# Turnings of x spread over the second layers, mixed blocks placed behind two doubles, a range check in two steps

## The chip, the cores and the metric

The kernel runs on one core of one Trainium2 chip. The metric is the device time of one execution in microseconds. Experiments that were sent together ran on one chip, beside runs of the kernel before on that chip; there were three such calls, on three chips.

## The reference

Causal attention with a learned decay bias over 8 batches, 8 heads, 576 tokens and head width 64, whose output (4608 tokens of width 512) goes through a top-1 mixture of 8 experts, each a two-layer network of width 1024:

```python
attn = softmax(scale * q @ k.T + min(-(cum_i - cum_j), 0), causal)
x = (attn @ v), heads joined                # (8, 576, 512)
for b in range(B):
    for s in range(S):
        fresh_e = argmax(x[b, s] @ w_gate)
        e = fresh_e if s == 0 or local_gate[b, s] < 0.5 else prev_e
        p = softmax(x[b, s] @ w_gate)
        out[b, s] = p[e] * (relu(x[b, s] @ w1[e]) @ w2[e])
        prev_e = e
```

All numbers are float32.

## The kernel before

The kernel first does attention (to about 302 us), sorting tokens by expert on the way, and then the expert stage, which is all that the change touches. Tokens of one expert are fetched in units: a "double" of 256 rows, a "single" of 128, or a "mixed" unit of two halves of 64 rows with two experts. The order of units is fixed; which expert a unit has is read from tables. There are 12 doubles (two of them "early", at the start), 10 singles and 4 mixed units.

```python
ORDER = "DMDSDMSDSDMSDSDMSDSDSDSS"
...
def turn_x(i, k):                       # transpose 128 rows of x
    x = xg.pop((i, k))
    ps = ps_x.tile([P, DK, P], F32, name="xp")      # pool of ONE buffer
    for c in range(DK):
        tr(ps[:, c, :], x[:, ...], ident)
    ...
    nc.vector.tensor_copy(xT[i][:, :, k * P : k * P + P], ps)
...
def layer1(i, first, last):
    ...
                else:                                # a mixed unit: 16 matmuls for each of 8 f
                    for swap in range(2):
                        for c in range(DK):
                            for h in range(2):
                                ...
                                mm(y[d, m], lhsT=w[h ^ swap][:, c, ...], rhs=xT[i][:, c, m], ...)
                for _ in range(nbs[i]):
                    tick()                           # counts steps; fires the hooks
...
def layer2(i, k, then):
    ps = ps_y.tile([P, D], F32, name="yp")
    for c in range(FK):                              # 8 chunks
        ...mm(ps, lhsT=hT[i][:, c, ...], rhs=wn[:, c, :], ...)
        if c == FK // 2 - 1:
            then()
        tick()
    y = gp.tile([P, D], F32, name="y", bufs=3)
    nc.vector.tensor_scalar_mul(y, ps, gate[i, k])
    nc.gpsimd.indirect_dma_start(out=..., in_=y, ...)

def turn(i):
    for k in range(2):
        turn_x(i, k)

def second(i):
    for k in range(nbs[i]):
        layer2(i, k, (lambda: turn_x(i + 2, k)) if nbs[i] == 2 else (lambda: turn(i + 2)))
...
turn(0)
layer1(0, 0, 4)
turn(1)
layer1(0, 4, FK)
...
for i in range(2 if ready else 0, NU):
    load(i)
    layer1(i + 1, 0, 4)
    fetch(i + 3)
    layer1(i + 1, 4, FK)
    second(i)
```

The first layer of unit i+1 comes before the second layer of unit i, and the rows of unit i+2 are turned inside the latter. Beside this, work of other kinds hangs on counted steps ("hooks"): the tail of attention and the first part of the last sorting at step 2, later parts at steps 6 to 16, and at step 60 a check that no softmax sum was out of range (three VectorE instructions, a matmul that adds over partitions, four small instructions).

Each float32 `mm` of the layers becomes two weight loads and two matmuls on the tensor engine (PE): in the trace the four mixed first layers, 4 x 128 calls, have 1024 weight loads and 1024 matmuls. So "x8" of a layer in a view stands for four calls, and a mixed first layer of 128 calls for 512 instructions.

## Time and profile before

| | |
|---|---|
| time | 882.5 us median (878.65 to 883.48, 3 runs) |
| time, with the run beside the kernel after | 880.58 us median (877.19 to 883.48, 4 runs) |
| span of the profiled run | 885.9 us |
| PE busy | 97% of the span |
| granted clock of PE, mean | 0.992 |
| DMA queue of instructions | 57 packets, 0.93 MB |

In the views, PE is the tensor engine's matmuls, PEld its weight loads, DVE VectorE, ACT ScalarE and POOL GpSimd. "PE hp L1129 <- issue: 7.0, 4, 3.7" means that PE, before the matmuls of line 1129 that write hp, waited 7.0 us in 4 waits, the longest 3.7, for nothing that the profile shows. In the chain of waits in order of time the columns are start, length and what ran. "hp" is a first layer, "yp" a second layer, "xp" the transposes of x, "bank" small matmuls of the hooks. A "block" is 256 instructions of PE, read from the traces: 57 packets of 16 KB came for the 14,268 instructions that the trace of the kernel before has of PE and its sequencer (250 each).

### The profile page before, as it was taken

What the parts mean: (1) busy time and instruction counts of PE and PEld (TensorE: products, weight loads), DVE (VectorE), ACT (ScalarE), POOL (GpSimd) and SP (SyncE); (2) the same over time, 40 slices, a digit from 0 to 9 for tenths busy, and PEclk for the clock granted to TensorE, in tenths of its full rate; (3) what the DMA queues carried; (4) which work ended last, traced back from release to release, by engine and by line L of the source; (5) the groups of instructions that cost most, each with busy time, mean ns of one, the idle gap of its engine ahead of it and who ended that gap; (6) DMA issues with size and microseconds to landing.
All of it is one profiled execution on the core that took longest, in us unless ns stands there. A gap on an engine that the chain in (4) does not pass through costs nothing.

```text
span 885.9 us, 17609 instructions
## 1 busy us (share of the span) xinstructions
PE 855.4 (97%) x7051; PEld 595.1 (67%) x7051; DVE 313.5 (35%) x837; ACT 185.4 (21%) x493; POOL 189.8 (21%) x289
## 2 busy tenths in 40 slices
PE   9999999999999999899998999999999999999996
PEld 7777776776767775486666567666667657676763
DVE  3656775778686665201111111111111111111110
ACT  5555555555455200000000000000000000000000
POOL 4322336237254114101010100101010101111000
PEclk9999999999999999999999999999999999999999
DMA  9165046653452518996797489776987689776000
GB/s 305 38 195 157 32 162 228 239 160 125 148 169 85 198 44 293 386 408 202 234 393 261 160 307 389 258 234 212 335 315 233 225 295 377 273 242 234 30 25 27
DMA packets 61403, 191.24 MB, mean 216 GB/s; under 512 B 7965, under 2 KB 9277, under 8 KB 61312
## 3 DMA queue, kind: packets, MB, share of 16 engines
q1 hardware_dynamic: 52272, 159.27, 52.1%
q0 software_dynamic: 8896, 30.47, 9.1%
q8 instruction: 57, 0.93, 0.4%
q10 hardware_dynamic: 144, 0.29, 0.1%
q14 instruction: 34, 0.28, 0.1%
HBM read 166.76 MB, written 23.76 MB: 215 GB/s over the span
## 4 chain that ended last, share of the span: by engine, by line
PE 93%; DVE 3%; issue 2%; POOL 1%; ACT 0%; POOLq 0%; DVEq 0%
PE yp L1146 30%; PE hp L1122 26%; PE ps L305 10%; PE o L353 10%; PE b L384 4%; PE o L377 4%; PE hp L1129 4%; PE xp L1097 2%; PE idle L269 1%; DVE xT L1100 1%; DVE r_u L921 0%; POOL x_rows L986 0%; DVE r_v L922 0%; ACT sc L311 0%; PE bank L917 0%
## 5 line engine op out<-in xcount | busy, mean ns | idle before, releaser
L1146 PE MATMUL yp<-w,hT 128*128 128x512 f32 (+1 forms) x480 | 202.0, 598 | 1.4 <-issue 1.4
L311 ACT ACTIVATE sc<-ps,bias 128x320 f32<-128x320 f32 (+4 forms) x448 | 160.5, 465 | 121.2 <-issue 62.9
L1122 PE MATMUL hp<-xT,w 128*128 128x128 f32 (+1 forms) x1088 | 172.2, 318 | 0.8 <-DVE xT L1100 0.8
L1122 PEld LDWEIGHTS hp<-xT,w 128*128 128x128 f32 x1088 | 157.5, 191 | 20.1 <-issue 7.8
L1146 PEld LDWEIGHTS yp<-w,hT 128*128 128x128 f32 (+1 forms) x480 | 79.8, 181 | 90.3 <-issue 88.4
L1153 POOL DMA_INDIRECT out_dram<-y,at x38 | 38.6, 1016 | 469.4 <-DVE y L1152 461.7
L1137 ACT ACTIVATE hT<-hp 128x512 f32<-128x512 f32 x38 | 22.7, 597 | 529.1 <-PE hp L1122 465.6
L305 PE MATMUL ps<-qk 64*128 64x320 f32 (+4 forms) x896 | 110.4, 380 | 3.6 <-DVE r_v L922 3.1
L1135 DVE TENSOR_SCALAR hT<-hp 128x512 f32<-128x512 f32 x38 | 26.2, 690 | 226.0 <-PE hp L1122 189.2
L353 PE MATMUL o<-sc,va 128*64 128x320 f32 (+4 forms) x896 | 101.3, 365 | 0.0
L317 POOL TENSOR_SCALAR_AFFINE_SELECT sc<-sc 128x256 f32<-128x256 f32 (+1 forms) x96 | 60.1, 626 | 152.5 <-ACT sc L311 103.6
L305 PEld LDWEIGHTS ps<-qk 64*128 64x128 f32 x896 | 72.2, 188 | 27.0 <-issue 7.0
L1146 PE MATMUL yp<-x,hT 128*128 128x512 f32 (+1 forms) x192 | 87.1, 604 | 0.0
L353 PEld LDWEIGHTS o<-sc,va 128*64 128x64 f32 x896 | 57.1, 137 | 42.7 <-issue 18.7
L1152 DVE TENSOR_SCALAR y<-yp,gate 128x512 f32<-128x512 f32 x38 | 28.5, 750 | 121.3 <-PE yp L1146 121.3
L1122 PE MATMUL hp<-xT,x 128*128 128x256 f32 x320 | 70.1, 380 | 0.0
L1122 PEld LDWEIGHTS hp<-xT,x 128*128 128x128 f32 x320 | 60.6, 190 | 11.1 <-issue 3.1
L340 DVE TENSOR_TENSOR sum<-sum,sc 128x640 f32<-128x640 f32 (+2 forms) x96 | 61.2, 637 | 9.8 <-POOL sc L317 4.9
L1100 DVE COPY xT<-xp 128x512 f32<-128x512 f32 x38 | 26.2, 691 | 101.7 <-PE xp L1097 101.6
L1146 PEld LDWEIGHTS yp<-x,hT 128*128 128x128 f32 (+1 forms) x192 | 34.1, 184 | 37.7 <-issue 37.6
L384 PE MATMUL b<-turn,xT 128*64 128x146 f32 x566 | 51.5, 291 | 0.6 <-issue 0.6
L986 POOL DMA_INDIRECT x_rows<-x,r_slot_i x40 | 43.4, 1086 | 11.4 <-issue 8.8
(156 smaller groups left out, 568.0 us busy)
## 6 DMA issues: line engine op xcount, KB each, us to landing
w<-in_w_dram SPq DMA_DIRECT2D x184, 512.0 KB, 7.1
x<-in_w_dram SPq DMA_DIRECT2D x56, 512.0 KB, 5.5
qk<-in_q_dram SPq DMA_DIRECT2D x32, 288.0 KB, 3.8
va<-in_vm_dram SPq DMA_DIRECT2D x35, 256.0 KB, 5.0
qk<-in_k_dram SPq DMA_DIRECT2D x31, 288.0 KB, 4.9
xg<-x_rows POOLq DMA_DIRECT2D x30, 293.0 KB
x_rows<-r_empty SPq DMA_DIRECT2D x6, 293.0 KB, 4.2
xg<-x_rows SPq DMA_DIRECT2D x4, 293.0 KB, 4.9
```

What stands on the lines that cost most here:

```text
L305: mm(ps[:, h, at : at + z - a], lhsT=kb[d, hp, KEYS[c] : KEYS[c] + P], rhs=qb[d, hp, a:z], start=True, stop=True)
L311: nc.scalar.activation(sc[:, h, at : at + z - a], ps[:, h, at : at + z - a], Act.Exp, bias=bias[:, i : i + 1], scale=scale)
L317: nc.gpsimd.affine_select(out=x, in_=x, compare_op=Alu.is_ge, fill=0.0, base=0, pattern=[[0, 2], [0, len(diag)], [1, P]], channel_multipli ...
L340: add(x, x, piece(n, c, 1), op=Alu.add)
L353: mm(o[DH * h : DH * h + DH, a - q0 : z - q0], lhsT=vas[b % 2][:, c, 2 * hp + h, :], rhs=w[:, h], start=(c == 0), stop=(c == (1, NF)[g]))
L377: mm(xs["o", 1][p : p + TL, i : i + 1], lhsT=w, rhs=one, start=True, stop=True)
L384: mm(ps[p : p + TL, t * 2 * HW : (t + 1) * 2 * HW], lhsT=xs["t", g][:, a : a + TL], rhs=w, start=True, stop=True)
L986: self.s.nc.gpsimd.indirect_dma_start(out=next(self.s.views)[:, :], out_offset=bass.IndirectOffsetOnAxis(ap=self.slot[:z, m : m + 1], axis=0),
L1122: mm(y, lhsT=w[0][:, c, f : f + P], rhs=xT[i][:, c, :], start=(c == 0), stop=(c == DK - 1))
L1129: mm(y[d, m], lhsT=w[h ^ swap][:, c, f + h * HALF : f + h * HALF + HALF], rhs=xT[i][:, c, m], start=(c == 0), stop=(c == DK - 1))
L1146: mm(ps[n * m : n * m + m, :], lhsT=hT[i][:, c, a : a + m], rhs=wn[:, c, :], start=(c == 0), stop=(c == FK - 1))
L1153: nc.gpsimd.indirect_dma_start(out=next(outs)[:, :], out_offset=bass.IndirectOffsetOnAxis(ap=at[i, k][:, 0:1], axis=0), in_=y[:, :], eleme ...
```

## The change

It has four parts. The transposes of a unit's two blocks no longer stand side by side, where the second waits for VectorE to empty the one buffer of `ps_x` (in the profile before 5.6 us in 6 waits). The mixed units go behind two doubles each. The range check is split into VectorE's part and PE's part six steps later. And at the start of the stage the tail of attention goes between the two transposes of the first unit, and those of the second unit are spread too (`tick(0)` runs the hooks of step 0 without counting a step).

```diff
-ORDER = "DMDSDMSDSDMSDSDMSDSDSDSS"
+ORDER = "DDMSSDDMSSDDMSSDDMSSDSDS"
...
-        hooks = [(2, lambda bank: (tail(bank), last.stages[0](bank))), (6, last.stages[1]), (11, last.stages[2]),
+        hooks = [(0, tail), (2, last.stages[0]), (6, last.stages[1]), (11, last.stages[2]),
...
-                 (60, lambda bank: in_range(tc, recs, sort.total, sort.ones, out_of, bank))]
+                 *((60 + 6 * i, lambda bank, f=f: f(bank)) for i, f in enumerate(check))]
...
-            if c == FK // 2 - 1:
-                then()
+            if c in then:
+                turn_x(*then[c])
             tick()
...
-            layer2(i, k, (lambda: turn_x(i + 2, k)) if nbs[i] == 2 else (lambda: turn(i + 2)))
+            layer2(i, k, {3: (i + 2, k)} if nbs[i] == 2 else {1: (i + 2, 0), 5: (i + 2, 1)})
...
-    turn(0)
+    turn_x(0, 0)
+    tick(0)
+    turn_x(0, 1)
     layer1(0, 0, 4)
-    turn(1)
-    layer1(0, 4, FK)
+    turn_x(1, 0)
+    layer1(0, 4, FK - 2 if nbs[0] == 2 else FK)
+    turn_x(1, 1)
+    if nbs[0] == 2:
+        layer1(0, FK - 2, FK)
...
-            layer2(1, k, lambda: turn(2 + k))
+            layer2(1, k, {1: (2 + k, 0), 5: (2 + k, 1)})
```

(The body of the check is only cut in two functions, `lanes` and `across`, of the same instructions.)

More of the change, by code (lines that the diff above doesn't have):

```diff
@@ L140 @@
         tables = sort.tables()
-        hooks = [(2, lambda bank: (tail(bank), last.stages[0](bank))), (6, last.stages[1]), (11, last.stages[2]),
+        check = in_range(main.enter_context(tc.tile_pool(name="g_sb", bufs=1)), nc, recs, sort.total, sort.ones, out_of)
+        hooks = [(0, tail), (2, last.stages[0]), (6, last.stages[1]), (11, last.stages[2]),
                  (13, last.stages[3]), (15, last.stages[4]),
@@ L463, in store_x, with in_range, lanes, across @@
                           tail[TL * h : TL * h + TL])
-@with_exitstack
-def in_range(ctx, tc, recs, halves, ones, out_of, bank):
-    nc = tc.nc
-    sb = ctx.enter_context(tc.tile_pool(name="g_sb", bufs=1))
-    flat = recs.rearrange("p n c -> p (n c)")
+def in_range(sb, nc, recs, halves, ones, out_of):
     k = NPAIR * 2 * NB
-    low = sb.tile([P, k], F32, name="g_low")
-    nc.vector.tensor_scalar(low, flat, 1.0 / SUM_MIN, None, Alu.is_le)
-    nc.vector.scalar_tensor_tensor(low, flat, 1.0 / SUM_MAX, low, Alu.is_ge, Alu.mult)
     count = sb.tile([P, 1], F32, name="g_count")
-    nc.vector.tensor_reduce(count, low, axis=AX, op=Alu.add)
-    total = bank(1)[0][:, :1]
-    nc.tensor.matmul(total, lhsT=ones, rhs=count, start=True, stop=True)
-    wrong, more = sb.tile([P, 1], F32, name="g_wrong"), sb.tile([P, 1], F32, name="g_more")
-    nc.vector.tensor_scalar(wrong, total, -1.0, float(P * k), Alu.mult, Alu.add)
-    nc.vector.tensor_scalar(more, halves, -float(SLOTS[2]), 0.0, Alu.add, Alu.max)
-    nc.vector.tensor_copy(out_of[:, 0:1], wrong)
-    nc.vector.tensor_tensor(out_of[:, 1:2], wrong, more, op=Alu.add)
+    def lanes(bank):
+        flat = recs.rearrange("p n c -> p (n c)")
+        low = sb.tile([P, k], F32, name="g_low")
+        nc.vector.tensor_scalar(low, flat, 1.0 / SUM_MIN, None, Alu.is_le)
+        nc.vector.scalar_tensor_tensor(low, flat, 1.0 / SUM_MAX, low, Alu.is_ge, Alu.mult)
+        nc.vector.tensor_reduce(count, low, axis=AX, op=Alu.add)
+    def across(bank):
+        total = bank(1)[0][:, :1]
+        nc.tensor.matmul(total, lhsT=ones, rhs=count, start=True, stop=True)
+        wrong, more = sb.tile([P, 1], F32, name="g_wrong"), sb.tile([P, 1], F32, name="g_more")
+        nc.vector.tensor_scalar(wrong, total, -1.0, float(P * k), Alu.mult, Alu.add)
+        nc.vector.tensor_scalar(more, halves, -float(SLOTS[2]), 0.0, Alu.add, Alu.max)
+        nc.vector.tensor_copy(out_of[:, 0:1], wrong)
+        nc.vector.tensor_tensor(out_of[:, 1:2], wrong, more, op=Alu.add)
+    return lanes, across
 @with_exitstack
@@ L1055, in bank, with tick @@
         return [ps_r.tile([P, 512], F32, name="bank") for _ in range(n)]
-    def tick():
+    def tick(n=1):
         nonlocal step
-        step += 1
+        step += n
         while hooks and hooks[0][0] <= step:
@@ L1155, in layer2 @@
             in_=y[:, :], element_offset=0, bounds_check=N - 1, oob_is_err=False, in_offset=None)
-    def turn(i):
-        for k in range(2):
-            turn_x(i, k)
     def second(i):
         for k in range(nbs[i]):
-            layer2(i, k, (lambda: turn_x(i + 2, k)) if nbs[i] == 2 else (lambda: turn(i + 2)))
+            layer2(i, k, {3: (i + 2, k)} if nbs[i] == 2 else {1: (i + 2, 0), 5: (i + 2, 1)})
     if ready:
@@ L1183, in experts @@
         for k in range(2):
-            layer2(0, k, lambda: None)
+            layer2(0, k, {})
         load(1)
         for k in range(2):
-            layer2(1, k, lambda: turn(2 + k))
+            layer2(1, k, {1: (2 + k, 0), 5: (2 + k, 1)})
         load(2)
```

## The prediction

> **What bounds the kernel now.** I read the page's first part, then the busy times by window, then who waited for whom on the tensor engine (PE) inside the second half, and last the chain of waits in order of time.
>
> Page, part 1, and the window of the expert stage (columns: window, length, then busy us of PE, PEld, DVE, ACT, POOL, then clock, DMA share, GB/s):
>
> ```profile
> PE 855.4 (97%) x7051; PEld 595.1 (67%) x7051; DVE 313.5 (35%) x837; ACT 185.4 (21%) x493; POOL 189.8 (21%) x289
> ...
> 302.00:886.00 584.00, 559.61 (x3285) 378.03 (x3282) 112.26 (x322) 22.84 (x39) 70.16 (x88) 0.99 0.69 246
> ```
>
> PE is the bound throughout; no other engine is near it. The change touches only the stage after 302 us. There PE is idle 584.0 - 559.6 = 24.4 us, of which the last 6.8 (879.08 to 885.9) are the closing scale, scatter and landing, which the change does not touch. So at most about 17.6 us of idle time are in reach, plus matmuls that run slow after an idle stretch. Who waited, for PE in that window (total us, times, longest):
>
> ```profile
> PE hp L1129 <- issue: 7.0, 4, 3.7
> PE xp L1097 <- DVE xT L1100: 5.6, 6, 1.7
> PE bank L480 <- DVE g_count L478: 2.2, 1, 2.2
> PE yp L1146 <- issue: 1.4, 2, 0.9
> PE hp L1122 <- DVE xT L1100: 0.8, 1, 0.8
> ```
>
> The reader is to see that these sum to 17.0 us and come in three kinds: first layers of mixed blocks (L1129) that wait for nothing the profile shows; transposes of x (L1097) and what follows them, waiting for VectorE's copy, because the PSUM pool of the transposes has one buffer; and the one matmul of the range check (L480). The chain in order of time shows the second and third kind (start, length, what):
>
> ```profile
> 366.60 0.45 PE xp L1097 x4
> ...
> 368.68 0.50 DVE g_count L478
> 369.17 0.04 issue
> 369.22 0.38 PE bank L480 x2
> 369.60 5.24 PE yp L1146 x8
> ...
> 484.82 3.67 issue
> 488.50 0.69 PE hp L1129 x15
> 489.18 5.33 PE yp L1146 x8
> ...
> 515.98 0.60 PE xp L1097 x4
> 516.58 0.02 issue
> 516.60 0.70 DVE xT L1100
> 517.30 0.04 issue
> 517.35 0.66 PE xp L1097 x4
> 518.00 3.58 PE yp L1146 x16
> ```
>
> The x8 after each long idle takes 5.24 and 5.33 us where the same x8 elsewhere takes 3.44: 1.8 and 1.9 us more.
>
> [...] the granted clock is 0.81 and 0.76 in the two 4 us windows from 368 us, and 0.74 and 0.83 from 488 us. [...] the first of these followed an idle of only 2.2 us. [...] The trace's queue of instructions shows 57 packets with 0.93 MB, 16.3 KB each[...]. It matters for L1129: between the starts of its four main stalls (394.34, 484.82, 592.29, 696.03 us) the windows count 1271, 1269 and 1268 matmuls and weight loads, which with about ten semaphore instructions is 5 x 256 each time. So I take these stalls for block boundaries whose next block had not landed, not for late weights. A mixed first layer has 512 such instructions in 8.1 us and uses a block in 4.1 us; a double's 128 take 13.8 us.
>
> **The change part by part.**
>
> *Turnings.* Where a single or mixed block turned a whole double at one place, the second four transposes waited for the copy: 515.98 to 518.00 = 2.02 us, against 2 x 0.44 = 0.88 when they are apart. Loss 1.14. The chain has it four times (357.85, 515.98, 620.65, 724.18). Now they stand after chunks 1 and 5: between them lie four chunks of 0.86 us, 3.4 us, against a copy of 0.70; after the second lie two chunks, 1.7 us, enough for its copy before the next first layer. Gain 4 x 1.14 = 4.6 us. Nothing is added; the number of transposes is the same.
>
> *Start of the stage.* Before: PE waits 0.79 + 0.78 + 0.17 + 1.69 = 3.4 us for VectorE there, and in between runs 2.3 us of small matmuls of the tail and the sorting. Now the tail's matmuls (0.90) fill the first copy's wait, but VectorE gets the tail's scaling and logits (about 1.9 us, 307.90 to 309.70) ahead of the second copy of x. I put the first L1122 at 306.2, against 304.98, with 0.9 of tail already done. The sorting's code (1.9 us of VectorE) then lies beside matmuls, and the two turnings of the next unit are apart, so that the scan no longer holds both. My walk ends the first unit's first layer at 322.3; before it ended at about 324.9 (338.7, the first second-layer matmul, less 13.8). Gain 2.5 us.
>
> *Range check.* The chain has VectorE's three steps from 367.88 to 369.17 with PE waiting 2.2 us. Now they start after step 60 and the matmul comes at step 66, six steps or some 5 us later, so the result is there. Gain 2.2, and 1.8 of slow clock after it: 4.0 us.
>
> *Order of blocks.* The work is the same: 12 double, 10 single, 4 mixed. By a replay of the weight loads (1.3 us for each of 8 pieces at the 410 GB/s shown when DMA is full, each piece behind the last reader of its buffer) no first layer waits for weights in either order; mixed blocks behind two doubles have some 28 us for their two sets, 21 of transfer. So what stays is the fetch of instructions. In the old order the first block boundary within the four mixed layers lay 1.7, 3.4, 2.4 and 1.2 us after its start, and the stall at the next was 1.31, 3.67, 1.59 and 0.38[...] Counting the built program's instructions on PE, the first boundary moves to about 2.5, 1.4, 0.2 and 3.1 us. Read off the old four, that gives 1.8, 0.5, 0.3 and 3.0 = 5.6 us, with 1.6 of slow clock, 7.2 in all, against 7.0 + 1.9 = 8.9. Gain 1.7 us; an estimate, and the weakest term.
>
> Sum: 4.6 + 2.5 + 4.0 + 1.7 = **12.8 us**. All of it is time in which PE, the bound, was idle or slow, so I take it off the span whole: 882.5 - 12.8 = 869.7, rounded to 869.5.
>
> **Rivals.**
> (a) *The mixed layers' stalls are late weights, and the new order removes them.* For it: DMA is saturated at 394 us. Against: their even spacing in instructions, and that DMA had idled just before 484 us (share 0.29 from 468 to 472). It would give the whole 8.9 instead of 1.7: some 862 us, over 2% faster.
> (b) *The fetch stalls grow.* A boundary's place is accidental, and four of 3.7 us with their slow clock would make 20 us instead of 8.9. That would eat the rest of the gain: about 880 us. For it: at the start of each mixed layer DMA is as full as before. Against: the mean of the old four is 1.7.
> (c) *A new wait at the start.* VectorE does the tail before the second half of x; if this takes 2 us more than I have, the start gains nothing: 872.
> (d) *The second turning comes too late* (two chunks before the next first layer). VectorE has 1.7 us for a 0.70 us copy; were it busy with another, some 0.3 us at each of eight places, 2.4 us in all. Its busy share there is 15%, so unlikely.
>
> **Range and chances.** The firm parts (turnings 4.6, check 4.0) are read from gaps in the trace; the start is +-1.5; the fetch stalls +-4. Runs of the kernel before spread by 4.8 us. So 864 to 875.5 holds it 8 times in 10. Faster by over 2% needs 17.7 us, nearly all the idle time in reach: 0.13. Slower by 2% has no mechanism large enough: 0.01. Within 2%: 0.86.
>
> **What would show it.** Right: in the expert stage PE waits for the xT copy only at the start (about 2 us) and nowhere in a second layer; no wait of L480's counterpart for the count; no x8 at 5.24 behind it; the first second-layer matmul near 336 us; mixed first layers still with "issue" waits of 4 to 8 us in sum, a multiple of 256 instructions apart. Wrong: those waits gone (rival a), or over 12 us (b); first layers of doubles waiting for weights; a wait of the xT copy at chunk 5.

## The result

The kernel after took 868.64 us median (866.97 to 870.49, 4 runs), against 880.58 us before on the same chip. Ratios here and below are the mean time of one kernel's fast runs over that of the other's fast runs of the same rounds, so not quite the ratio of the medians: 0.9866, 95% interval 0.9819 to 0.9914. The prediction was 869.5, range 864 to 875.5.

The profiled run of the kernel after: page part 1,

```profile
PE 847.9 (98%) x7051; PEld 594.0 (69%) x7051; DVE 314.1 (36%) x837; ACT 185.5 (21%) x493; POOL 188.5 (22%) x289
```

and who waited for whom on PE in the expert stage (total us, times, longest):

```profile
PE hp L1133 <- issue: 4.2, 3, 2.3
PE hp L1126 <- DVE xT L1104: 1.9, 1, 1.9
```

PE is still the bound, with 7.5 us less of busy time for the same matmuls. Of the five waits that added up to 17.0 us, two are left (line numbers moved by four), 6.1 us in sum. The chain of waits of the kernel after, in order of time, at the check, at the four mixed first layers, and in a single's second layer:

```profile
363.48 1.73 PE hp L1126 x8
365.20 0.12 PE bank L482 x2
...
411.83 2.26 issue
...
453.97 0.44 PE xp L1101 x4
454.40 3.44 PE yp L1150 x8
457.84 0.44 PE xp L1101 x4
458.27 1.72 PE yp L1150 x4
459.99 13.81 PE hp L1126 x64
...
514.82 0.28 issue
...
611.56 7.62 PE hp L1133 x256
...
720.10 1.69 issue
```

The check's matmul (L482) runs inside a first layer without a wait. A double that is turned inside a single's second layer costs 0.44 + 0.44 us and no wait, and the first layer behind it (459.99) starts at once. The third mixed layer runs 7.62 us without a stop, the others stop for 2.26, 0.28 and 1.69 us.

The two profiled spans differ by 20.5 us, more than the 11.9 us between the medians. The first transpose of x starts at 302.09 us before and at 298.03 us after: 4 us of the difference lie in attention, which the change does not touch. Conclusions are drawn from the timed runs and from single gaps, not from that difference.

At the start of the stage something did not go as predicted. The chain of waits of the kernel after has there

```profile
301.40 0.61 DVE xT L1104
302.01 0.04 issue
302.06 7.13 PE hp L1126 x24
```

and its busy times by window (window, length, busy us of PE, PEld, DVE, ACT, POOL, then clock, DMA share, GB/s) have

```profile
302.06:309.20 7.14, 7.14 (x26) 5.85 (x27) 1.61 (x10) 0.87 (x2) 0.00 (x0) 0.76 0.05 19
```

The 24 matmuls take 7.13 us where 24 x 0.216 = 5.2 are usual (64 take 13.81), and the granted clock is 0.76 there: behind the remaining wait of 1.9 us the clock dropped (to 0.50 from 303.11 us on, for 3.413 us).

### The profile page after: what moved, and what is told of

It reads as the page before. It is cut to its first block, busy times and chain, and to the rows that moved or that the text cites. A ratio compares the mean times of both kernels' runs of the same rounds, so it can differ in the third digit from the quotient of the medians.

```text
span 865.4 us, 17612 instructions
## 1 busy us (share of the span) xinstructions
PE 847.9 (98%) x7051; PEld 594.0 (69%) x7051; DVE 314.1 (36%) x837; ACT 185.5 (21%) x493; POOL 188.5 (22%) x289
## 4 chain that ended last, share of the span: by engine, by line
PE 97%; DVE 1%; issue 1%; POOL 0%; POOLq 0%; DVEq 0%
PE yp L1150 30%; PE hp L1126 28%; PE ps L306 11%; PE o L354 11%; PE b L385 5%; PE o L378 4%; PE hp L1133 4%; PE xp L1101 2%; PE idle L270 1%; DVE r_u L925 0%; DVE r_v L926 0%; PE bank L921 0%; PE bank L936 0%; PE bank L954 0%; PE bank L955 0%
## 5 line engine op out<-in xcount | busy, mean ns | idle before, releaser
L1150 PE MATMUL yp<-w,hT 128*128 128x512 f32 (+1 forms) x528 | 221.1, 594 | 0.0
L1126 PE MATMUL hp<-xT,w 128*128 128x256 f32 (+1 forms) x1088 | 193.8, 339 | 1.9 <-DVE xT L1104 1.9
L1126 PEld LDWEIGHTS hp<-xT,w 128*128 128x128 f32 x1088 | 173.2, 192 | 26.4 <-issue 7.8
L1150 PEld LDWEIGHTS yp<-w,hT 128*128 128x128 f32 (+1 forms) x528 | 88.0, 180 | 100.5 <-issue 99.5
L1150 PE MATMUL yp<-x,hT 128*128 128x512 f32 (+1 forms) x144 | 64.8, 595 | 0.0
L1126 PE MATMUL hp<-xT,x 128*128 128x128 f32 (+1 forms) x320 | 50.1, 317 | 0.0
L1126 PEld LDWEIGHTS hp<-xT,x 128*128 128x128 f32 x320 | 46.1, 191 | 5.8 <-issue 2.6
L385 PEld LDWEIGHTS b<-turn,xT 128*64 128x64 f32 x566 | 38.6, 137 | 7.8
```

The source lines that it names most:

```text
L385: mm(ps[p : p + TL, t * 2 * HW : (t + 1) * 2 * HW], lhsT=xs["t", g][:, a : a + TL], rhs=w, start=True, stop=True)
L1126: mm(y, lhsT=w[0][:, c, f : f + P], rhs=xT[i][:, c, :], start=(c == 0), stop=(c == DK - 1))
L1150: mm(ps[n * m : n * m + m, :], lhsT=hT[i][:, c, a : a + m], rhs=wn[:, c, :], start=(c == 0), stop=(c == FK - 1))
```

## The experiments

Three questions: what each part is worth by itself; whether the mixed layers stop for instructions or for late weights; and whether what is left can be had.

| run | call | median us | runs | before, median us | ratio to before | 95% interval |
|---|---|---|---|---|---|---|
| kernel after | first | 868.64 | 4 | 880.58 | 0.9866 | 0.9819 to 0.9914 |
| e1 turnings alone | A | 876.31 | 6 | 881.48 | 0.9947 | 0.9922 to 0.9973 |
| e2 check alone | A | 878.55 | 6 | 881.48 | 0.9972 | 0.9939 to 1.0006 |
| e3 order alone | A | 885.58 | 6 | 881.48 | 1.0052 | 1.0024 to 1.0080 |
| e4 start alone | A | 880.99 | 6 | 881.48 | 0.9993 | 0.9964 to 1.0022 |
| e5 all but the order | B | 876.77 | 6 | 884.41 | 0.9913 | 0.9889 to 0.9936 |
| e6 after, padded | B | 880.72 | 4 | 884.41 | 0.9953 | 0.9925 to 0.9980 |
| e7 after, tail split | B | 874.57 | 6 | 884.41 | 0.9879 | 0.9856 to 0.9902 |
| e8 after, laced | B | 875.39 | 6 | 884.41 | 0.9895 | 0.9873 to 0.9917 |
| e9 after, again | C | 878.20 | 6 | 882.68 | 0.9933 | 0.9908 to 0.9958 |
| e10 after, halves | C | 869.09 | 5 | 882.68 | 0.9835 | 0.9809 to 0.9861 |
| e11 after, tail split, again | C | 874.10 | 6 | 882.68 | 0.9900 | 0.9871 to 0.9928 |
| e12 after, halves and tail split | C | 867.28 | 5 | 882.68 | 0.9807 | 0.9782 to 0.9833 |

All were correct.

### e1: the turnings alone

The edit, on the kernel before, is the part of the diff that concerns `then` in `layer2`, `second` and the early units.

> The kernel before with the spread turnings in the second layers alone. My theory: the four waits of 0.79 us for the copy of xT in second layers go, with some 0.35 us each of matmuls that could not overlap, 4 x 1.14 = 4.6 us off the span; the wait for the range check (about 2.2 us) and the waits of the mixed first layers (before: 7.0 us) stay. Rival (a copy that comes too late behind chunk 5): xT waits appear before first layers, and less than 2 us are gained.

Measured: 0.9947, 4.7 us of 881. Who waited for whom on PE in the expert stage:

```profile
PE xp L1097 <- DVE xT L1100: 2.5, 2, 1.7
PE bank L480 <- DVE g_count L478: 0.5, 1, 0.5
```

The four waits of 0.79 us are gone; the two of 0.8 and 1.7 us that are left are at the start of the stage, which this kernel has unchanged. No wait for xT appears ahead of a later first layer, so the rival falls. The size agrees with the predicted 4.6 us. (The check's wait shrank to 0.5 us as well, presumably since the turning next to it moved; so 1.7 us of these 4.7 may be the check's, and what remains is still within the interval.)

### e2: the check in two steps alone

The edit is the two `hooks` lines of the check and the cut of its body.

> The kernel before with the range check in two steps alone. My theory: PE's wait of 2.2 us for the count goes and with it the slow stretch behind it (8 matmuls in 5.24 us become 3.44): 4.0 us in all. Rival (the clock was low for another reason): only 2.2 us go, and the 8 matmuls still take about 5 us.

Measured: 0.9972, 2.5 us, with an interval from a gain of 5.4 to a loss of 0.5 us. The chain of waits at the check:

```profile
361.75 3.44 PE yp L1150 x8
365.19 1.73 PE hp L1126 x8
366.92 0.12 PE bank L482 x2
```

The wait is gone, and the x8 that took 5.24 us in the kernel before takes 3.44. So the mechanism is as predicted; the timed runs do not tell 4.0 from 2.2 us.

### e3: the order alone

```diff
-ORDER = "DMDSDMSDSDMSDSDMSDSDSDSS"
+ORDER = "DDMSSDDMSSDDMSSDDMSSDSDS"
```

> The kernel before with the new order of blocks alone. My theory: the mixed first layers' waits fall from 7.0 to about 4 us, as in the kernel after, because the instruction block boundaries lie at the same places as there; but in this order two singles stand ahead of two doubles, so a whole double is turned at one place nine times instead of four, 5 x 1.14 = 5.7 us more. In sum 0 to 3 us slower than before, or equal within noise. Rival (weights came late and the order cures that): no waits of mixed layers at all, 8.9 less 5.7 = 3 us faster.

Measured: 1.0052, 4.6 us slower. Who waited for whom on PE:

```profile
PE xp L1097 <- DVE xT L1100: 9.5, 11, 1.7
PE hp L1129 <- issue: 4.2, 3, 2.2
```

The order without the spread turnings makes nine waits for the copy of xT in second layers, as expected (the other two are the start's), because two singles ahead of two doubles turn a whole double each. The mixed layers' waits are 4.2 us in three, the same sum as in the kernel after: so they are not cured by the order, and the rival (late weights, cured by the order) falls. The loss is a little over the 0 to 3 us that I expected. The order pays, if at all, only together with the spread turnings.

### e4: the start alone

The edit is the last part of the diff and the split of the first hook.

> The kernel before with the new start of the expert stage alone (tail's matmuls between the two turnings of the first unit, the second unit's turnings apart). The profile after showed PE's waits there down from 3.4 to 1.9 us, but the one that is left is followed by 24 matmuls in 7.1 us instead of 5.2. My theory now: about 1 us gained or nothing, far less than the 2.5 us of the prediction; one wait of 1.9 us ahead of the first layer with slow matmuls behind it. Rival (the slow matmuls were of that one profile): 1.5 to 2.5 us gained, and those 24 in about 5.2 us.

Measured: 0.9993, 0.6 us, interval from a gain of 3.2 to a loss of 1.9 us. Its profile shows the same wait of 1.9 us, and behind it 24 matmuls in 7.13 us, as in the kernel after. So the start gave about nothing, as far as the timed runs can tell.

### e5: all but the order

The kernel after with the old `ORDER`.

> The kernel after with the old order of blocks. The instruction blocks end where they did before the change. My theory: the mixed first layers wait as before, 5 to 9 us with slow matmuls, against 4.2 in the kernel after; so it lies 1 to 5 us above the kernel after, 872 or so. Rival (order does nothing at all): equal to the kernel after.

Measured: 0.9913, 7.7 us. Within the noise it equals the sum of the three single parts: 4.7 + 2.5 + 0.6 = 7.8 us. Its mixed layers waited 6.3 us in its profile. The kernel after had 0.9866 in its first measurement and 0.9933 in its second (e9), one better and one worse than 0.9913, on other chips. What the order adds beside the spread turnings is therefore not settled: between a gain of 4 and a loss of 2 us by these means alone.

### e6: a shift of half a block of instructions

```diff
     turn_x(0, 1)
+    if ready:
+        pad = bank(1)[0]
+        for _ in range(32):
+            mm(pad[:, :1], lhsT=ident, rhs=ident[:, :1], start=True, stop=True)
     layer1(0, 0, 4)
```

> The kernel after with 32 one-column matmuls (128 PE instructions) put into the idle ahead of the first first layer; results unchanged. They shift every later block of 256 instructions by half a block. Theory of instruction fetch: in the kernel after the four mixed layers waited 2.26, 0.28, 0 and 1.69 us at block boundaries. Here the boundaries in those layers move 2 us earlier (or 2 us later by the next block): about 0 to 0.5, 2 to 3.5, 1 to 2 and 0.2 to 0.6 us. Rival of late weights: the same waits as in the kernel after, at the same time after each layer's start, the first the longest and the second below 0.5. Span: the padding itself costs about nothing, as PE idles there, and may save up to 1.9 us by keeping the clock up.

The chain of waits at the four mixed first layers:

```profile
420.42 0.12 issue
420.54 5.59 PE hp L1133 x183
...
527.57 3.04 issue
...
631.68 1.77 issue
...
734.58 1.05 issue
```

The stops are now 0.12, 3.04, 1.77 and 1.05 us: the first layer, which stopped longest in the kernel after, hardly stops (its 0.12 us lie 2.4 us into the layer, while its block boundaries lie 0.6 and 4.7 us in), the second stops longest, and the third, which had run through, stops. Weights, loads and their order are the same in both kernels; only the count of instructions ahead of them changed. This is what instruction fetch predicts (0 to 0.5, 2 to 3.5, 1 to 2, and 0.2 to 0.6, the last a little under what was measured), and late weights cannot do it.

The kept traces settle it more directly. Each holds the packets of DMA queue 8, the queue of instructions, with their times. In the kernel before, the four main stops end 1.44, 1.47, 1.28 and 1.32 us after such a packet of 16 KB has landed; in the kernel after the three end 1.47, 1.28 and 1.40 us after one. Over all profiles with such stops there are 33 longer than 0.2 us in mixed first layers; all end 1.17 to 1.48 us after a packet, and all lie at the same place in the count of PE's recorded instructions, modulo 256 (in the kernel before the four main stops end 1280 instructions apart each time). So PE waited for the block; why the packet came late (the DMA share is 0.99 in the stop of 3.04 us here) was not tested.

My expectation of the cost was a miss: the 32 matmuls took 9.5 us (64 pairs of weight load and matmul, 112 ns apart at first; the clock dropped to half 4.4 us into them and stayed there for 10.2 us, with the pairs 213 ns apart; over the 9.5 us PE was busy throughout, and the mean granted clock is 0.72). So the kernel is slow for that reason, and its time says nothing of the stops.

### e7 and e11: VectorE's part of the tail behind the second copy

```diff
-    return lambda bank: back(NPAIR - 1, 1, bank(1)[0])
+    def tail_rows(bank):
+        xs["tail"] = bank(1)[0]
+        rows(NPAIR - 1, 1, xs["tail"])
+
+    def tail_rest(bank):
+        divide(NPAIR - 1, 1, xs["tail"])
+        logits(B - 1)
+
+    return tail_rows, tail_rest
...
-        hooks = [(0, tail), (2, last.stages[0]), ...
+        hooks = [(0, tail[0]), (1, tail[1]), (2, last.stages[0]), ...
```

> The kernel after with VectorE's part of the tail (scaling and logits, 1.9 us) moved behind the second copy of x; its matmuls stay where they are. My theory: the wait of 1.9 us ahead of the first layer shrinks to about 0.7 us and the slow clock behind it (24 matmuls in 7.1 us instead of 5.2) goes: 1.2 + 1.9 = 3 us faster than the kernel after. Rival (the slow clock does not hang on that wait): 1.2 us.

> The kernel after with VectorE's part of the tail behind the second copy of x, again, now beside the kernel after on one chip, since the first run of it had another chip and more waits of mixed layers. Theory: from the first transposition to the first second-layer matmul 33.3 us, as in its first run, against 36.1 in the kernel after when the clock drops there and 34.4 when it does not; 1 to 3 us faster than the kernel after. Rival: what is gained at the start is lost again in waits and slow clock behind it, equal.

Measured: 0.9879 in call B and 0.9900 in call C, where the kernel after had 0.9933. In call C the mean is 874.80 against 877.52 us, 2.7 us less, though the six runs of each overlap (872.99 to 878.71 and 874.57 to 879.34). In both profiles the wait ahead of the first layer is 0.8 us, and from the first transpose to the first second-layer matmul it takes 33.27 us, against 36.06 or 34.37 in the kernel after. This agrees with the expected 1 to 3 us; it does not tell the 3 us of the theory of e7 from the 1.2 us of its rival.

### e8: each mixed first layer laced into a second layer

Both layers are made to be stepped; after each eighth of the mixed first layer two chunks of the preceding double's second layer follow:

```diff
                 for _ in range(nbs[i]):
                     tick()
+                for _ in range(2):
+                    next(beside, None)
...
-        layer1(i + 1, 0, 4)
-        fetch(i + 3)
-        layer1(i + 1, 4, FK)
-        second(i)
+        work = second(i)
+        beside = work if i + 1 < NU and units[i + 1][0] == "mixed" and nbs[i] == 2 else iter(())
+        layer1(i + 1, 0, 4, beside)
+        fetch(i + 3)
+        layer1(i + 1, 4, FK, beside)
+        list(work)
```

> The kernel after with each mixed first layer laced into the second layer of the double ahead of it: after each eighth of it, two chunks of the second layer. The same matmuls and loads; but 256 instructions now last about 8 us instead of 4. Theory of instruction fetch: the waits of the mixed first layers go (4.2 us in the kernel after), 3 to 5 us faster. Rival of late weights: the waits stay or only move, since the weights are needed as early as before.

Who waited for whom on PE in the expert stage, all of it:

```profile
PE hp L1126 <- DVE xT L1104: 1.9, 1, 1.9
PE yp L1152 <- issue: 0.9, 1, 0.9
```

A piece of the chain in order of time:

```profile
410.63 1.91 PE yp L1152 x4
412.54 1.08 PE hp L1133 x32
```

The mixed layers' waits are gone altogether, with the same matmuls and the same weights. But the time did not fall as expected: its ratio of 0.9895 lies between the two of the kernel after (0.9866 and 0.9933, on other chips; call B had no run of it). The x4 of the second layer takes 1.91 us here and 1.72 in the kernel after, and an eighth of the mixed layer 1.08 against 7.62 / 8 = 0.95. That is 0.32 us for each of 8 steps, 2.6 us a layer, 10 us for four, by an estimate from these pieces: more than the 4.2 us that the waits took in the kernel after. Each step has a change from 128-wide to 64-wide matmuls and back; the trace shows the 0.32 us, not what takes them. So the waits go as the theory of instruction fetch says, and the cure is too dear. (Lacing also gives the weights of the mixed layer more time, so that it is e6 that tells fetch from late weights.)

### e9: the kernel after, again

No edit.

> The kernel after, unchanged, so that the next three have it on their own chip, and to see how far its waits differ from one profile to the next. Theory: ratio to before 0.983 to 0.990; in the expert stage again only the 1.9 us wait at the start and the mixed first layers' waits, at the same block boundaries (the first and last mixed layer the longest), but of other sizes, 4 to 8 us in sum; none to three stretches of slow clock of 1.7 us each.

Measured: 878.20 us, ratio 0.9933 (0.9908 to 0.9958), half the gain of the first measurement, outside the expected ratio of 0.983 to 0.990, and outside the range of 864 to 875.5 us that I had predicted for the time. Its profile stops 5.7 us in mixed layers (2.63, 0.44, 0 and 2.61, the same layers as before, of other size) and 1.3 us at the first second layer. Another part is the clock. Each run records its mean granted clock; (1 - clock) x time, averaged over runs, is an estimate of the time lost to it (it also counts slow stretches in which PE waits anyhow, as at the end of each profile): 3.9 us in the four runs of the first measurement, 6.9 us in these six (clock 0.990 to 0.997), 4.3 us in the kernel before on this chip. So of the 8.8 us between the two means (877.52 and 868.69) some 3 go to the clock and 2.8 to longer stops, if the two profiles stand for the runs; the kernel before, too, is slower here, by 3.4 us in the mean (883.88 against 880.46). And here the same wait of 1.9 us at the start left the clock alone (it is 1.00 from 302.06 to 320 us; chain in order of time; 7.13 us in the kernel after):

```profile
305.22 5.45 PE hp L1126 x24
```

### e10: halves

As e8, but with only one break: the first of the two passes of the double's second layer goes between the halves of the mixed first layer.

```diff
+        work = second(i)          # yields once after each pass
         layer1(i + 1, 0, 4)
         fetch(i + 3)
+        if i + 1 < NU and units[i + 1][0] == "mixed" and nbs[i] == 2:
+            next(work)
         layer1(i + 1, 4, FK)
-        second(i)
+        list(work)
```

> The kernel after with the first pass of the preceding double's second layer put between the two halves of each mixed first layer, so that no block of 256 instructions lies in a mixed layer alone, with two changes between 64-wide and 128-wide matmuls a layer instead of the sixteen of the laced kernel, which cost it about 2 us a layer. Theory of instruction fetch: waits of mixed layers below 2 us in sum; the added changes cost 0.5 us a layer, 2 us in all; 2 to 6 us faster than the kernel after. Rival (the cost of laced matmuls does not go by the number of changes): equal to the kernel after or slower.

Measured: 869.09 us, 0.9835. Who waited for whom on PE in the expert stage, all of it:

```profile
PE hp L1126 <- DVE xT L1104: 1.9, 1, 1.9
PE yp L1150 <- issue: 0.3, 1, 0.3
```

The chain at the first mixed layer:

```profile
410.02 0.05 issue
410.07 1.86 PE hp L1133 x55
411.94 3.63 PE yp L1150 x8
```

A block of 256 instructions never lies in a mixed layer alone any more, and at the block boundaries no stop is left (0.05 to 0.12 us remain some 2.3 us into a mixed layer, away from them, as in other profiles). Against the kernel after in the same call the mean falls from 877.52 to 869.15 us, 8.4 us: more than the expected 2 to 6 us and than the 5.7 us of stops. The clock stays up as well (lost to it: 2.3 us against 6.9), which can account for the rest.

### e12: halves and the split tail together

> Both changes together. Theory: their gains add, 4 to 8 us faster than the kernel after, ratio to before about 0.980. Rival: 0.985 or more.

Measured: 867.28 us (five runs within 1.3 us), ratio to before 0.9807 (0.9782 to 0.9833): the fastest ratio of all, and faster than the kernel after of the same call by 867.15 / 877.52 = 0.988, 10.4 us in the means. The expected 4 to 8 us were less than that. Whether it is over 2% faster than the kernel before is not settled, as the interval holds 0.98. The clock costs 1.2 us here.

## Why the prediction was right, point by point

- **Time.** 868.64 us against 869.5 predicted. The second measurement of the same kernel (878.2 us, ratio 0.9933 against 0.9866) lies outside the range: the range was made of the mechanisms and of the runs before the change, and had too little room for the clock, whose cost differed by 3 us between the two measurements (3.9 and 6.9 us), and for stops of varying size. The prediction started from 882.5 us, and on that chip the kernel before stood at 882.68, so a slower chip is no excuse. That the first measurement came within 1 us is in part luck: the three parts that were measured alone add up to 7.8 us, where the prediction has 4.6 + 4.0 + 2.5 = 11.1. The direction and "within 2%" hold in both.
- **The waits.** The prediction sums 17.0 us and puts them in three kinds. The 1.4 us of "PE yp L1146 <- issue" belong to none of them; they are the stop left open below.
- **Turnings, 4.6 us.** Right: e1 shows the waits gone and 4.7 us, of which up to 1.7 may be the check's.
- **Range check, 4.0 us.** Right in mechanism (e2 shows the wait and the slow matmuls gone); 2.5 us measured, with 4.0 inside the interval.
- **Start, 2.5 us.** This is the term that was mis-sized. I had the wait right (1.9 us; the text said about 2) but walked on at full clock, although two steps further on I counted slow clock behind a wait of 2.2 us. The walk has 336.1 - 302.1 = 34.0 us from the first transpose of x to the first second-layer matmul. In three profiles with that start (the kernel after, e4, e8) the stretch from the first transpose to the first second-layer matmul takes 36.06 us, in three others (e5, e9, e10) 34.37; before it took 36.60. So it gains 0.5 or 2.2 us; e4 measured 0.6. Where the clock dropped, the traces of the kernels before and after have it at 0.50 for 3.413 us each time (longer only in the last stretch, which runs past the end of the span): after from 303.11 us, 1.05 us behind the end of the wait; before from 223.70, 370.47 and 489.94 us. These starts in the kernel before are 43 and 35 times 3.413 us apart. In the 3.41 us ahead of such a stretch PE was busy for 45% in the kernel after (1.52 us), and for 82, 37 and 42% in the kernel before. Behind the same wait of 1.9 us the 24 matmuls took 7.13 us in the kernel after, e4 and e8, and 5.45 us in e9. What decides which of the two comes was not tested.
- **Order, 1.7 us.** Predicted stops 1.8, 0.5, 0.3 and 3.0; measured 2.26, 0.28, 0 and 1.69, and in e9 2.63, 0.44, 0 and 2.61. The mechanism, blocks of instructions, is shown by e6 (stops move with the count), by the packets that land before each stop ends, and, with less force, by e8 and e10 (stops go when a block lasts longer). Between the stops at 411.83, 514.82 and 720.10 us the trace of the kernel after has 1280 and 2816 PE instructions, those of its sequencer included: 5 and 11 times 256. That a later boundary waits longer was my estimate from four stops of the kernel before (1.31, 3.67, 1.59 and 0.38 us, with the first boundary 1.7, 3.4, 2.4 and 1.2 us into the layer); a cause was not tested. The size of a stop is not settled by its place alone: with the old order five profiles (before, e1, e2, e4, e5) have 6.0 to 7.8 us in sum, with the new one five (after, e3, e7, e9, e11) 4.2 to 7.4, on average 6.8 and 5.3. Whether the order gains at all beside the other parts stays open (e5 against the two measurements of the kernel after).
- **Rivals.** (a) late weights: refuted by e3, e6 and the packets. (b) growing stops: not seen, 4.2 and 5.7 us against 7.0. (Its "about 880" should be 882.5: 20 us instead of 8.9 eat the other 11.1 whole.) (c) a new wait at the start: half right, through the clock. (d) the second turning too late: not seen in any profile.

Left open: a stop of PE of 0.3 to 1.9 us in total just after the first second-layer matmuls, for nothing that the profile shows, in the kernel before and in e5 to e12 but not in the first profile of the kernel after nor in e1 to e4. It is not at a block boundary, and I have no explanation that a run tested.

## What to carry to other kernels

When the bounding engine waits "for nothing", count its instructions between the waits. Here an even spacing in instructions, not in time, marked instruction fetch (1280 each of three times before, 1280 and 2816 after), and shifting the count by half a block tested it in one run (e6: stops of 0.12, 3.04, 1.77 and 1.05 us instead of 2.26, 0.28, 0 and 1.69); the trace's packets of the instruction queue, landing 1.2 to 1.5 us before the end of each wait here, show it without one. What cured it here was not to move such dense code (e3 kept 4.2 us of stops) but to break it up with instructions that last longer, in few and large pieces (e10, no stop left at a block boundary, ratio 0.9835): in the many small pieces of e8 each step took about 0.32 us more by the estimate above (ratio 0.9895). And a wait of about 2 us on the tensor engine cost up to about twice its length here, as the clock dropped behind it: behind 1.9 us (kernel after, 24 matmuls in 7.13 us; 5.45 in e9) and 2.2 us (before, 8 matmuls in 5.24 us instead of 3.44). It did not drop behind 1.9 us in e9, nor does the x8 behind the 3.04 us of e6 show it (3.63 us; 5.33 behind the 3.67 us of the kernel before).
